# Down's weight sums formed block by block during gate and up, kept in DRAM, and loaded ready-made

## The chip, the cores and the metric

One Trainium2 chip, one core of it. The metric is the device time of one execution in microseconds (us); several executions are timed and their median is given. The kernel's engines are TensorE (PE, with its weight loads shown apart as PEld), VectorE (DVE), ScalarE (ACT), GpSimd (POOL) and SyncE (SP), whose queue issues nearly all DMAs.

## The reference

x is 2048 x 576, in float32. `a` is a linear attention of 32 heads of 18, `b` a gated MLP with 4608 inner columns, and the output mixes them row by row:

```python
g = sigmoid((x * gate_w).sum(-1, keepdims=True))
q, k, v = heads(x @ wqkv); pq, pk = phi(q), phi(k)      # phi(t) = (t + 1 if t > 0 else exp(t)) + 1e-6
kv = einsum("bhsd,bhse->bhde", pk, v); z = pk.sum(s)
a = merge((pq @ kv) / (pq . z + 1e-6)) @ wo
h = gelu(x @ w_gate) * (x @ w_up)                       # 2048 x 4608
b = h @ w_down                                          # 2048 x 576
out = g * a + (1 - g) * b
```

## The kernel before

Attention comes first, up to about 285 us of the profiled execution. Then follow two long stages with which the change deals.

**Gate and up** (to 1067.6 us). x and both weight matrices are cut in two halves along each side, and each product of 2 x 2 blocks is made with seven block products in place of eight. The work is 72 *chains*: for one pair of column blocks (n, 0 to 17), gate or up, and one half of the rows (p), the seven products. A product is one *step* of seven matmuls of 512 columns. Two neighbouring chains are interleaved: a *frame* is seven steps, `FRAME = 1, 7, 5, 3, 6, 2, 4`, of which steps 0, 4 and 5 belong to the chain that starts and steps 1, 2, 3 and 6 to the one before. The code of a step is issued in program order to all engines, and behind it whatever the dictionary `plan` holds for (frame, step); `put(frame, i, ...)` fills it. So `plan` sets the order on every queue. In it stand, among others:
- `fetch_at`: the load of the next raw weight blocks (768 KB into `wraw`, the front of the tile `stage`) and, behind it in the program, `weight_sums`: four subtractions on POOL (L373) that wait for this load.
- `split_at`: each block is split into a high part on ACT (L868) and a low part on POOL (L869, L870) for the float32r matmuls.
- `extras`: sums of finished h blocks (DVE, L996 and L999), stored to `h_d` in DRAM; `a`-side pieces go to `ha_d` and come back later.

Product 5 (`s5`, step 2 of a frame) ends with an ACT copy (L971) and a DVE addition that reads the bank `c` (L973 or L976); product 4 (`s4`, step 6) goes on accumulating in `c`.

**Down** (1067.6 us to the end). The table `DOWN` has 26 products; each has an h operand (`h_d`, a sum of h blocks) and a weight operand `v`, which is a block of w_down (a name of two digits) or a sum of blocks (a letter). Each product is done in three chunks, which makes 78 *units* of 36 matmuls of 288 columns, 18 in each half of a unit. A product marked `c` goes on in the PSUM banks of the one before. Behind a product's third chunk its banks are read into `acc` by DVE (L1403). Around each unit u the program issues, in this order: the first half's matmuls (and reads); `h_make(u + 3)`, which splits the raw h block (ACT L1240 or L1237, then DVE L1241 or L1238) and then loads another raw block into the buffer that this frees; `w_make(u + 3)`, which splits the weight operand (ACT L1203, POOL L1204); `w_sums`; the second half. At some u, `later()` does one more piece of the last chain's h sums (DVE L996, L999), with its stores and loads.

The class `Weights` keeps w_down blocks of 128 x 864 in up to 18 buffers `vt`. `fetch` loads blocks some units ahead (L1187), `sums(j)` forms the sums for unit j from them on DVE or POOL (L1198), and some sums stay in a buffer for later sums:

```python
        for name, x, op, y in DOWN[m].made:
            ...
            eng = nc.gpsimd if j > 4 and (c == 1 or c == 2 and m % 2) else nc.vector
            eng.tensor_tensor(self.tile(name, c), a, b, OP.add if op == "+" else OP.subtract)
```

Raw h blocks of 768 KB have three buffers (`raw_at`), and from a point in `later()` a fourth, `e123`, which until then serves the last chain's sums.

Of the kernel before, what the change touches and what calls it, by code (L numbers as in the profile page):

```python
# [8 lines left out]
F32 = mybir.dt.float32  # L9
# [76 lines left out]


class Product:

# [25 lines left out]
def tile_gated_mix(ctx, tc, xt, xs, xn, wk, wv, wq, wo, wgu, wdn, cst, out):  # L115
# [33 lines left out]
    class Scope:  # L149
        def __init__(self):  # L150
            self.stack = ExitStack()
# [994 lines left out]
    def raw_view(v):  # L1146
        return f32(v).rearrange("p (g c) -> p g c", g=3)

    wd = [wd_view(v) for v in (xf[:, 6144:7872], xf[:, 7872:9600], xf[:, 9600:11328], xf[:, 15936:17664])]
    hb = [h_view(v) for v in (xf[:, :3072], xf[:, 3072:6144], wf[1][:, :3072], xf[:, 12864:15936])]  # L1150
    raw_at = [raw_view(v) for v in (xf[:, 11328:12864], wf[0][:, :1536], wf[0][:, 1536:3072])] + [e123]
    raw_free = deque([0])
    vt = [stage[:, i * 864:(i + 1) * 864] for i in range(5)]

    class Weights:


        def __init__(self):
            self.tasks, self.last, self.at, self.free = [], {}, {}, list(range(15))
            used = {}  # L1160
            for j, (m, c) in enumerate(UNITS):
                d = DOWN[m]
                for name in [x for made in d.made for x in (made[1], made[3], made[0])] + [d.v]:
                    used.setdefault((name, c), []).append(j)
            self.spans = {}
            for (name, c), js in used.items():
                first = prev = js[0]
                for j in js[1:] + [10 ** 6]:
                    if j - prev > 9 and name.isdigit() or j == 10 ** 6:
                        self.spans.setdefault((name, c), []).append((first, prev))  # L1170
                        first = j
                    prev = j
            self.fetches = sorted((a, name, c) for (name, c), v in self.spans.items() for a, _ in v if name.isdigit())

        def tile(self, name, c):
            return vt[self.at[name, c]]

        def drop(self, j):
            for (name, c), v in self.spans.items():
                if (name, c) in self.at and any(b == j for _, b in v):  # L1180
                    self.free.append(self.at.pop((name, c)))

        def fetch(self, upto):
            while self.fetches and self.fetches[0][0] <= upto:
                _, name, c = self.fetches.pop(0)
                self.at[name, c] = self.free.pop(0)
                nc.sync.dma_start(self.tile(name, c).rearrange("p (g c) -> p g c", g=3),  # L1187
                                  wdn[2 * int(name[0]) + int(name[1])][:, 3 * c:3 * c + 3])

        def sums(self, j):  # L1190
            m, c = UNITS[j]
            for name, x, op, y in DOWN[m].made:
                dead = [k for k in (x, y) if any(b == j for _, b in self.spans[k, c]) and k != DOWN[m].v
                        and not any(k in (q[1], q[3]) for q in DOWN[m].made[DOWN[m].made.index((name, x, op, y)) + 1:])]
                a, b = self.tile(x, c), self.tile(y, c)
                self.at[name, c] = self.at.pop((dead[0], c)) if dead else self.free.pop(0)
                eng = nc.gpsimd if j > 4 and (c == 1 or c == 2 and m % 2) else nc.vector
                eng.tensor_tensor(self.tile(name, c), a, b, OP.add if op == "+" else OP.subtract)  # L1198

        def make(self, j):  # L1200
            m, c = UNITS[j]
            w, src = wd[j % 4], self.tile(DOWN[m].v, c)
# [4 lines left out]
    weight = Weights()  # L1207
    AHEAD = 3

    def w_sums(j, ahead=AHEAD):  # L1210
        if j < len(UNITS):
            weight.fetch(j + ahead)
            weight.sums(j)

    def w_make(j):
        if j < len(UNITS):
            weight.make(j)

# [89 lines left out]
    for n in range(3, NF2):  # L1308
        split_at(4 * n - 3, 0, GATE, *ALL)
        fetch_at(4 * n - 3, 5, n, UP)  # L1310
        split_at(4 * n - 1, 0, UP, *ALL)
        if n < NF2 - 1:
            fetch_at(4 * n - 1, 5, n + 1, GATE)
    for n, k in enumerate((1, 6, 2, 7, 5, 3, 4)):
# [15 lines left out]
    for do in late.pop(0):  # L1330
        put(LAST, 4, do)
    E_FREE = late.index([])
    late.pop(E_FREE)
# [33 lines left out]
    acc = dp.tile([128, 4, 2, 4, 288], F32, name="acc")  # L1367
    vt += [dp.tile([128, 864], F32, name=f"vt{i}") for i in range(10)]
    for v, k in ((f, 2), (sx, 1)):
        v = v.rearrange("p a b -> p (a b)")  # L1370
        vt += [v[:, i * 864:(i + 1) * 864] for i in range(k)]
    sets, set_of = [], {}
# [36 lines left out]
    def later():  # L1409
        if late:  # L1410
            for do in late.pop(0):
                do()
            if len(late) == 18 - E_FREE:
                raw_free.append(3)
            if not late:
                weight.free.extend((15, 16, 17))

    weight.fetch(7)
    acc_load(1)
    for u in range(len(UNITS)):  # L1420
        unit(u, 0)
        h_make(u + 3)
        w_make(u + 3)
        if not u:
            w_sums(4)
        w_sums(u + 5)
        unit(u, 1)
        if u in LATER:
            later()
        if u in (5, 12, 20):  # L1430
            acc_load((0, 2, 3)[(5, 12, 20).index(u)])
# [74 lines left out]
```

## Time and profile before

| | us |
|---|---|
| median of 3 runs (1453.39 to 1453.88) | 1453.6 |
| the profiled execution | 1452.77 |
| its span, first to last instruction | 1451.0 |
| DVE busy in the span | 989.0 |
| ACT busy | 640.8 |
| POOL busy | 823.6 |

The times of the prediction's rows are microseconds from the start of the span; the execution's own time is 1.77 us longer than its span, and the median of the runs is 0.83 us above the profiled execution. PE is busy for 1437.3 us of the span. A busy PE is not always PE at its pace, since a matmul's end is modelled; so the gaps are also read from the starts of the matmuls.

### The profile page before, as it was taken

Reading aid. Unit: us, or ns where it says so; the run is one execution under the profiler, and the core shown is the slowest. Engines: PE = TensorE matmul, PEld = TensorE weight load, DVE = VectorE, ACT = ScalarE, POOL = GpSimd, SP = SyncE. Lnnn points to the kernel's source line nnn. Section 1 sums busy time; section 2 is a strip of 40 time slices with the busy share of each in tenths; the row PEclk is TensorE's granted clock in tenths of the full one; section 3 lists DMA queues with packets and bytes.
Section 4 is the critical chain, followed back from the end, with each engine's and each line's share of the span. In section 5 each row is a group of like instructions: output and inputs, shape, how many; then the busy total and the mean of one; then the engine's idle time right before and its main releaser. Section 6 shows DMA issues by size and latency. Waiting matters only on the chain. (4 is left out here: it accounts for less than half of the span.)

```text
span 1451.0 us, 21113 instructions
## 1 busy us (share of the span) xinstructions
PE 1437.3 (99%) x8096; PEld 1281.7 (88%) x8096; DVE 989.0 (68%) x1115; ACT 640.8 (44%) x863; POOL 823.6 (57%) x511
## 2 busy tenths in 40 slices
PE   9999999999999999999999999999999999999999
PEld 9999899988888888888888888888889999999999
DVE  7887898343745538465374753647478989999794
ACT  7554656443333443333433334433345445444542
POOL 1674543365554545535445454455147968799895
PEclk9999999999999999999999999999999999999999
DMA  7574486663634436344263533535888787767771
GB/s 259 158 210 132 155 266 199 236 234 118 224 119 141 156 127 218 131 160 151 103 210 131 192 134 104 194 131 205 304 286 318 249 318 253 235 229 249 246 240 52
DMA packets 123925, 282.13 MB, mean 194 GB/s; under 512 B 12008, under 2 KB 39208, under 8 KB 122672
## 3 DMA queue, kind: packets, MB, share of 16 engines
q1 hardware_dynamic: 121232, 275.80, 55.7%
q10 hardware_dynamic: 2592, 4.98, 0.9%
q8 instruction: 63, 1.03, 0.3%
q14 instruction: 38, 0.31, 0.1%
HBM read 182.20 MB, written 98.50 MB: 193 GB/s over the span
## 5 line engine op out<-in xcount | busy, mean ns | idle before, releaser
L854 PE MATMUL bank<-xo,wg 128*128 128x512 f32 x1764 | 415.4, 389 | 0.5 <-ACT bank L943 0.5
L854 PE MATMUL bank<-xo,wu 128*128 128x512 f32 x1715 | 403.4, 389 | 0.0
L854 PEld LDWEIGHTS bank<-xo,wg 128*128 128x128 f32 x1764 | 330.8, 188 | 69.6 <-ACT bank L943 0.9
L854 PEld LDWEIGHTS bank<-xo,wu 128*128 128x128 f32 x1715 | 321.8, 188 | 67.0 <-DVE bank L976 0.2
L1393 PE MATMUL bank<-xo 128*128 128x288 f32 x2124 | 285.5, 295 | 5.4 <-DVE acc L1403 5.4
L1393 PEld LDWEIGHTS bank<-xo 128*128 128x128 f32 x2124 | 282.0, 188 | 6.9 <-DVE acc L1403 4.1
L373 POOL TENSOR_TENSOR stage<-stage 128x384 f32<-128x384 f32 x132 | 134.7, 1041 | 164.7 <-DMA stage<-wgu 162.0
L943 ACT ACTIVATE bank<-bank 128x512 f32<-128x512 f32 x139 | 80.9, 582 | 242.4 <-PE bank L854 237.2
L869 POOL TENSOR_TENSOR wg<-stage,wg 128x768 fp32r<-128x768 f32 (+3 forms) x41 | 73.9, 1802 | 126.9 <-ACT wg L868 122.3
L1204 POOL TENSOR_TENSOR xo<-vt,xo 128x864 fp32r<-128x864 f32 x42 | 124.2, 2965 | 27.9 <-ACT xo L1203 26.5
L1204 POOL TENSOR_TENSOR xo<-stage,xo 128x864 fp32r<-128x864 f32 x32 | 96.0, 3005 | 66.2 <-ACT xo L1203 66.2
L869 POOL TENSOR_TENSOR wu<-stage,wu 128x768 fp32r<-128x768 f32 (+2 forms) x36 | 74.0, 2056 | 86.2 <-ACT wu L868 81.9
L976 DVE TENSOR_TENSOR bank<-bank,mid 128x512 f32<-128x512 f32 x36 | 25.1, 697 | 143.2 <-ACT mid L971 143.1
L1393 PE MATMUL bank<-xo,wu 128*128 128x288 f32 x684 | 93.8, 295 | 1.4 <-DVE acc L1403 1.4
L1393 PEld LDWEIGHTS bank<-xo,wu 128*128 128x128 f32 x684 | 91.4, 188 | 1.9 <-DVE acc L1403 1.1
L973 DVE TENSOR_TENSOR f<-bank,mid 128x512 f32<-128x512 f32 x18 | 12.5, 692 | 115.0 <-ACT mid L971 110.8
L971 ACT ACTIVATE mid<-bank 128x512 f32<-128x512 f32 x71 | 42.4, 597 | 101.7 <-PE bank L854 90.3
L781 PEld LDWEIGHTS pair<-kw,p 128*128 128x128 f32 x448 | 60.8, 189 | 1.0
L781 PE MATMUL pair<-kw,p 128*128 128x288 f32 x448 | 61.4, 295 | 0.0
L531 PE MATMUL bank<-xo,qw 128*128 128x512 f32 (+1 forms) x231 | 55.7, 392 | 0.0
L1241 DVE TENSOR_TENSOR xo<-wg,xo 128x1536 fp32r<-128x1536 f32 x18 | 48.9, 2718 | 5.2 <-ACT xo L1240 5.2
L531 PEld LDWEIGHTS bank<-xo,qw 128*128 128x128 f32 (+1 forms) x231 | 41.9, 183 | 10.0
(257 smaller groups left out, 2190.6 us busy)
## 6 DMA issues: line engine op xcount, KB each, us to landing
wg<-h_d SPq DMA_DIRECT2D x41, 768.0 KB, 4.2
stage<-wgu SPq DMA_DIRECT2D x33, 768.0 KB, 5.0
h_d<-sx SPq DMA_DIRECT2D x72, 256.0 KB, 2.7
xo<-h_d SPq DMA_DIRECT2D x23, 768.0 KB, 4.2
h_d<-mid SPq DMA_DIRECT2D x64, 256.0 KB, 3.4
h_d<-e SPq DMA_DIRECT2D x63, 256.0 KB, 4.7
vt<-wdn SPq DMA_DIRECT2D x29, 432.0 KB, 5.2
e<-h_d SPq DMA_DIRECT2D x13, 768.0 KB
```

The lines of the kernel that those rows point to most:

```text
L373: nc.gpsimd.tensor_tensor(o, a, b, OP.subtract)
L531: nc.tensor.matmul(ps[:wa.shape[1]], wa, xa, start=(k == 0), stop=(k == len(ops) - 1), skip_group_check=g == 4)
L781: nc.tensor.matmul(y[:, i, :288], p[:, 5 * a + g], KW[g][:, wl, i * 288:(i + 1) * 288], start=(n == 0), stop=(n == 13))
L854: nc.tensor.matmul(ps, w_, x_, start=start and i == 0, stop=i == 6, skip_group_check=not start)
L869: nc.gpsimd.tensor_tensor(w[:, i, 3:5], src[:, :, 0:2], f32(w[:, i, 0:2]), OP.subtract)
L943: nc.scalar.activation(o, src, AF.Copy)
L971: nc.scalar.activation(d_sum, d, AF.Copy)
L973: nc.vector.tensor_tensor(es[3], ps["c"], d_sum, OP.add)
L976: nc.vector.tensor_tensor(d, ps["c"], d_sum, OP.add)
L1204: nc.gpsimd.tensor_tensor(w[:, 1], src, f32(w[:, 0]), OP.subtract)
L1241: nc.vector.tensor_tensor(h[:, 1], raw, f32(h[:, 0]), OP.subtract)
L1393: nc.tensor.matmul(y, h[:, hl, g, t * 128:(t + 1) * 128], w[:, wl, g * 288:(g + 1) * 288], start=first and c == 0 and n == 0, stop=c == NK ...
```

## The change

Each sum of w_down blocks is made during gate and up, for all products at once, in pieces. w_down's rows are in nine groups (`g`) of which a unit's weight operand uses three. For each g, a table `SUMS` of 48 steps makes 13 loads of 128 x 288 (144 KB; ten are pieces of blocks, three are sums that come back), forms 18 sums in five small buffers, and stores each to a DRAM tile `v_d` of its name. A word `4:2=0+1` means: at step 4, buffer 2 becomes buffer 0 plus buffer 1; `5:2>s` stores buffer 2 as `s`; `5:0<30` loads. The nine groups follow one another from frame 4 to frame 65. That adds 117 loads, 162 stores and 162 sums there, 79 of the sums on DVE and 83 on POOL. The buffers are the rear of `stage` and a new tile `fifth`.

In down, `Weights` is gone. Each unit's operand is loaded from `wdn` or `v_d` into one of five buffers (`v_fetch`), five units ahead, issued behind `w_make` of the unit that had the buffer. The room of the other `vt` buffers goes to raw h blocks: `e123` is no longer one of them, and five buffers `hr` come in one by one behind units 5, 6, 8, 10 and 11.

Two smaller edits: from n = 3 on, `weight_sums` is issued three steps behind its load and no longer right behind it; the first down loads of the old kernel (blocks for units up to 3 at frame LAST - 4, step 6) become the operands of units 0 to 4 at the same place.

```diff
+SUMS = """
+0:0<11 0:1<31 0:3<21 4:2=0+1 5:2>s 5:0<30 6:4=3-1 7:4>y 7:3<10 9:2=0+2 10:2>t 11:4=4-0 12:4>r 13:2=3+2
...
+"""
...
+    v_d = {name: dram.tile([128, NF2 // 2, 288], F32, name=f"v_d{name}") for name in "yrvwzoxkmqpnsjutAl"}
...
+    fifth = stages.tile([128, 320], F32, name="fifth")
...
-    raw_at = [raw_view(v) for v in (xf[:, 11328:12864], wf[0][:, :1536], wf[0][:, 1536:3072])] + [e123]
+    raw_at = [raw_view(v) for v in (xf[:, 11328:12864], wf[0][:, :1536], wf[0][:, 1536:3072])]
...
-    class Weights:
...
+    class Sums:
+        def __init__(self, g):
+            self.g, self.slots = g, [stage[:, c:c + 288] for c in range(3072, 4224, 288)] + [fifth[:, :288]]
...
+        def do(self, what, eng):
+            o, s, g = self.slots[int(what[0])], self.slots, self.g
+            if what[1] == "<":
+                nc.sync.dma_start(o, v_at(what[2:])[:, g])
+            elif what[1] == ">":
+                nc.sync.dma_start(v_at(what[2:])[:, g], o)
+            else:
+                eng.tensor_tensor(o, s[int(what[2])], s[int(what[4])], OP.add if what[3] == "+" else OP.subtract)
+
+    def v_fetch(j):
+        if j < len(UNITS):
             m, c = UNITS[j]
...
+            nc.sync.dma_start(vt[j % 5].rearrange("p (g c) -> p g c", g=3), v_at(DOWN[m].v)[:, 3 * c:3 * c + 3])
+
+    def w_make(j):
+        if j < len(UNITS):
+            w, src = wd[j % 4], vt[j % 5]
             nc.scalar.activation(w[:, 0], src, AF.Copy)
             nc.gpsimd.tensor_tensor(w[:, 1], src, f32(w[:, 0]), OP.subtract)
-            self.drop(j)
...
+            v_fetch(j + 5)
...
+        for m, frame, blocks in ((GATE, 4 * n - 3, (n, UP)), (UP, 4 * n - 1, (n + 1, GATE))):
+            split_at(frame, 0, m, *ALL)
+            if blocks[0] < NF2:
+                put(frame, 5, lambda at=blocks: nc.sync.dma_start(wraw, wgu[at]))
+                put(frame + 1, 1, lambda: weight_sums(wraw, tsum))
+    for g in range(NF2 // 2):
+        one = Sums(g)
+        for at, what in one.tasks():
+            frame, i = divmod(28 + 48 * g + at, 7)
+            eng = nc.gpsimd if i > 3 or frame % 2 == 0 == i else nc.vector
+            put(frame, i, lambda one=one, what=what, eng=eng: one.do(what, eng))
...
-    for frame, i, do in ((LAST - 4, 6, lambda: weight.fetch(3)), (LAST - 2, 1, lambda: h_direct(0)),
+    for frame, i, do in ((LAST - 4, 6, lambda: [v_fetch(j) for j in range(5)]), (LAST - 2, 1, lambda: h_direct(0)),
...
-                         (LAST + 1, 6, lambda: (h_make(2), weight.sums(3)))):
+                         (LAST + 1, 6, lambda: h_make(2))):
...
-    vt += [dp.tile([128, 864], F32, name=f"vt{i}") for i in range(10)]
...
+    raw_at += [raw_view(dp.tile([128, 1536], F32R, name=f"hr{i}")) for i in range(5)]
...
-    weight.fetch(7)
+    MORE = 5, 6, 8, 10, 11
     acc_load(1)
     for u in range(len(UNITS)):
         unit(u, 0)
         h_make(u + 3)
         w_make(u + 3)
-        if not u:
-            w_sums(4)
-        w_sums(u + 5)
         unit(u, 1)
+        if u in MORE:
+            raw_free.append(3 + MORE.index(u))
+            h_load()
```

How the order moves, at three places. On DVE in down around unit 18, before: the split of an h block (L1241), a weight sum (L1198), one of the last chain's sums (L996), the next split, the reads of a product (L1403).

```order
L1403 SCALAR_TENSOR_TENSOR acc<-bank,gate,acc 128x288 x2
L1241 TENSOR_TENSOR wu<-xo,wu 128x1536
L1198 TENSOR_TENSOR vt_8788<-stage,vt_8788 128x864
L996 TENSOR_TENSOR e_3256<-e_3256,r 128x512
L1241 TENSOR_TENSOR xo<-wg,xo 128x1536
L1403 SCALAR_TENSOR_TENSOR acc<-bank,gate,acc 128x288 x2
L1241 TENSOR_TENSOR xo<-wg,xo 128x1536
```

And now, where L1222 is the split, L1005 the sum of h blocks and L1386 the read:

```order
L1386 SCALAR_TENSOR_TENSOR acc<-bank,gate,acc 128x288 x2
L1222 TENSOR_TENSOR wu<-hr_9246,wu 128x1536
L1005 TENSOR_TENSOR e_3274<-e_3274,r 128x512
L1222 TENSOR_TENSOR xo<-xo 128x1536
L1386 SCALAR_TENSOR_TENSOR acc<-bank,gate,acc 128x288 x2
L1222 TENSOR_TENSOR xo<-hr_9249,xo 128x1536
```

The weight sum is gone from between them; nothing else has changed its place there.

On SP's queue in the last two frames of gate and up, before: weights of the last chain (`xo<-wp_d`), pieces of the `a` side to be kept (`ha_d`), and the raw h block of unit 2 (`wu<-h_d`).

```order
L1318 DMA xo<-wp_d_97 128x640
L1011 DMA ha_d8x<-sx 128x512
L1011 DMA ha_d8y<-f 128x512
L1318 DMA xo<-wp_d_97 128x640
L1011 DMA ha_d_151<-sx 128x512
L1223 DMA wu<-h_d_100 128x1536
L1318 DMA xo<-wp_d_97 128x640
L1011 DMA ha_d_152<-f 128x512
```

And now, with L1305 for the weights, L1020 for the pieces, L1204 for the raw h block:

```order
L1305 DMA xo<-wp_d_97 128x640
L1020 DMA ha_d8x<-sx 128x512
L1020 DMA ha_d8y<-f 128x512
L1191 DMA stage<-wdn 128x864
L1305 DMA xo<-wp_d_97 128x640
L1020 DMA ha_d_151<-sx 128x512
L1204 DMA wu<-h_d_100 128x1536
L1305 DMA xo<-wp_d_97 128x640
L1020 DMA ha_d_152<-f 128x512
```

A load of 432 KB (L1191, the operand of unit 6) has come in; that of unit 5 stands a few rows ahead of these, that of unit 7 a few rows behind.

On DVE in a frame of gate and up (frame 35), before: the last chain's sums, then the addition that reads bank `c` (L973).

```order
L996 TENSOR_TENSOR sx<-bank,sx 128x512
L999 TENSOR_TENSOR e_3256<-f,e_3256 128x512
L996 TENSOR_TENSOR e_3256<-e_3256,r 128x512
L973 TENSOR_TENSOR e_3256<-bank,mid 128x512
L983 TENSOR_TENSOR e_3256<-bank,mid 128x512
L996 TENSOR_TENSOR sx<-r,f 128x512
```

And now, L982 being that addition and L1186 a sum of the new table:

```order
L1005 TENSOR_TENSOR sx<-bank,sx 128x512
L1008 TENSOR_TENSOR e_3274<-f,e_3274 128x512
L1186 TENSOR_TENSOR stage<-stage 128x288
L1005 TENSOR_TENSOR e_3274<-e_3274,r 128x512
L982 TENSOR_TENSOR e_3274<-bank,mid 128x512
L992 TENSOR_TENSOR e_3274<-bank,mid 128x512
L1186 TENSOR_TENSOR fifth<-fifth,stage 128x288
L1005 TENSOR_TENSOR sx<-r,f 128x512
```

Two sums of 128 x 288 have come in, one of them two rows ahead of the addition.

More of the change, by code (lines that the diff above doesn't have):

```diff
@@ L1150, in tile_gated_mix @@
     hb = [h_view(v) for v in (xf[:, :3072], xf[:, 3072:6144], wf[1][:, :3072], xf[:, 12864:15936])]
-    raw_at = [raw_view(v) for v in (xf[:, 11328:12864], wf[0][:, :1536], wf[0][:, 1536:3072])] + [e123]
+    raw_at = [raw_view(v) for v in (xf[:, 11328:12864], wf[0][:, :1536], wf[0][:, 1536:3072])]
     raw_free = deque([0])
     vt = [stage[:, i * 864:(i + 1) * 864] for i in range(5)]
-    class Weights:
[L1158 to L1190, printed above, removed]
-            m, c = UNITS[j]
[L1192 to L1202, printed above, removed]
@@ new lines, in v_at, with tasks @@
+    def v_at(name):
+        return wdn[2 * int(name[0]) + int(name[1])] if name.isdigit() else v_d[name]
+    class Sums:
+        def __init__(self, g):
+            self.g, self.slots = g, [stage[:, c:c + 288] for c in range(3072, 4224, 288)] + [fifth[:, :288]]
+        def tasks(self):
+            for word in SUMS.split():
+                at, what = word.split(":")
+                yield int(at), what
+        def do(self, what, eng):
[6 more added lines that the diff above has]
+                eng.tensor_tensor(o, s[int(what[2])], s[int(what[4])], OP.add if what[3] == "+" else OP.subtract)
@@ L1215, in w_make @@
-    def w_make(j):
-        if j < len(UNITS):
-            weight.make(j)
+            v_fetch(j + 5)
     DIRECT = 3
@@ L1331, in tile_gated_mix @@
         put(LAST, 4, do)
-    E_FREE = late.index([])
-    late.pop(E_FREE)
+    late.remove([])
     for k, src, (frame, i), (back, j) in kept:
@@ L1412, in later @@
                 do()
[L1413 to L1416, printed above, removed]
-    weight.fetch(7)
+    MORE = 5, 6, 8, 10, 11
     acc_load(1)
```

17 lines of the change are left out of this document (3 added, 14 removed).

## The prediction

> **What bounds the kernel now.** I read the page's head first, then each stage's busy times, then who waits for PE's banks, then PE's timeline.
>
> ```profile
> span 1451.0 us, 21113 instructions
> PE 1437.3 (99%) x8096; PEld 1281.7 (88%) x8096; DVE 989.0 (68%) x1115; ACT 640.8 (44%) x863; POOL 823.6 (57%) x511
> ...
> 600.00:690.00 90.00, 90.00 (x399) 74.53 (x398) 49.71 (x66) 33.72 (x48) 45.67 (x35) 1.00 0.46 152
> ...
> 1150.00:1200.00 50.00, 47.76 (x357) 47.01 (x356) 44.85 (x28) 24.47 (x24) 33.49 (x12) 1.00 0.87 311
> ...
> PE bank L1393 <- DVE acc L1403: 6.8, 8, 1.8
> ...
> PE bank L854 <- DVE bank L976: 0.9, 1, 0.9
> ```
>
> The columns of a stage row are length, then busy PE, PEld, DVE, ACT, POOL, the granted clock, the DMA share and GB/s. Only PE bounds: in gate and up it is busy 90.00 of 90.00 us with DVE and POOL half idle, so nothing there can be gained. In down DVE is busy 44.85 of 50 us and PE loses 2.24. The rows of the waits name the cause: eight times PE waits for DVE's read of a product (L1403). PE's timeline gives the price:
>
> ```profile
> 1067.60 9.65 PE L1393 MATMUL bank<-xo 128*128 128x288 f32 x72
> ...
> 1157.35 2.61 PE L1393 MATMUL bank<-xo,wu 128*128 128x288 f32 x18 [0.58 <-DVE acc L1403]
> 1160.78 2.65 PE L1393 MATMUL bank<-xo,wu 128*128 128x288 f32 x18 [0.83 <-DVE acc L1403]
> ...
> 1414.40 14.40 PE L1393 MATMUL bank<-xo 128*128 128x288 f32 x108
> 1428.64 4.91 PE L1393 MATMUL bank<-xo,wu 128*128 128x288 f32 x36
> 1433.39 14.40 PE L1393 MATMUL bank<-xo 128*128 128x288 f32 x108
> ```
>
> Undisturbed, 108 matmuls take 1428.64 - 1414.40 = 14.24 us, so a unit of 36 takes 4.75 and half a unit 2.37. From 1157.35 to 1160.78 half a unit took 3.43: the stall cost 1.06, 0.23 more than its idle 0.83. Eight stalls make 6.8 + 8 x 0.23 = 8.6 us. The whole checks it: from the first unit (1067.60) to the 76th (1433.39) there are 2700 matmuls, at 14.24 per 108 they take 356.0, and they took 365.8: 9.8 us lost. The 1.2 between I cannot place and do not count.
>
> **What the change takes away in down.** Is a weight sum the reason that DVE reads late?
>
> ```profile
> 1148.90 2.77 DVE L1241 TENSOR_TENSOR wu<-xo,wu 128x1536 fp32r<-128x1536 f32 x1
> 1151.59 2.91 DVE L1198 TENSOR_TENSOR vt<-stage,vt 128x864 f32<-128x864 f32 x1
> 1154.42 0.68 DVE L996 TENSOR_TENSOR e<-e,r 128x512 f32<-128x512 f32 x1
> 1155.02 1.75 DVE L1241 TENSOR_TENSOR xo<-wg,xo 128x1536 fp32r<-128x1536 f32 x1
> 1156.69 0.93 DVE L1403 SCALAR_TENSOR_TENSOR acc<-bank,gate,acc 128x288 f32<-128x288 f32 x2
> ...
> 1067.00:1451.00 384.00, 68.64 (x27) 89.47 (x27) 1.00 0.69 240
> ...
> 1059.27 1.47 ACT L1237 ACTIVATE xo<-xo 128x1536 fp32r<-128x1536 f32 x1
> ...
> 1224.68 3.61 DVE L1238 SCALAR_TENSOR_TENSOR wu<-wg,wu 128x1536 fp32r<-128x1536 f32 x1
> 1228.22 2.55 DVE L999 TENSOR_TENSOR r<-sx,r 128x512 f32<-128x512 f32 x1
> 1230.68 1.78 DVE L1403 SCALAR_TENSOR_TENSOR acc<-bank,gate,acc 128x288 f32<-128x288 f32 x4
> ```
>
> At the stall of 1157.35 DVE had no gap from 1148.90 on. Without the 2.91 us sum the first reads would have begun 2.9 us sooner, where 0.82 was missing. The stage row (length, DVE, POOL) is of L1198 alone: 27 sums with 68.6 us on DVE and 27 with 89.5 on POOL, all of which leave. Over the 26 products that is 2.6 us of DVE for each product of 14.24; the longest stall is 1.8. So I take the 8.6 back, less what other late work leaves. The worst place is the product with two destinations for each bank (1230.68, four reads in 1.78 us), with no sum right ahead of it but a piece of the last chain's sums (2.55). There, at worst and without the sums, ACT's copy (1.47), the split beside POOL (3.61), the piece beside POOL (2.55), the reads of two banks (1.78), the next split bare (1.75, as at 1155.02) and the third bank's two reads (0.9) end 12.1 us after the unit began in which the copy stands; PE wants that bank after 2.5 units, 11.9. I leave 0.2 there and 0.4 for the rest: 0.6 in all. The bounds are 0 and 4.3 (half the stalls stay). Down: +8.0.
>
> **What it adds in down.** 78 operand loads of 432 KB in place of 48 block loads; with a raw h block (768 KB) each 4.75 us, 1.229 MB or 259 GB/s. Units 5 to 11 (33 us) also bring five extra h blocks and one `acc_load` (1.18 MB): 5.1 MB, 154 GB/s more, 413 in all.
>
> ```profile
> 1110.00:1120.00 10.00, 10.00 (x78) 10.00 (x77) 9.36 (x9) 5.01 (x6) 8.54 (x3) 1.00 1.04 403
> ```
>
> 403 GB/s is the fullest that this trace shows for so long; 413 leaves a backlog of 0.3 MB, under 1 us, and the last chain's pieces perhaps 2 us more. An operand is loaded five units (23.7 us) ahead, an h block three units (14.2) less about 5 for DVE's split and SP's turn. Hidden; without cover the cost is the backlog itself. A page speaks against this: the Trainium skill, "DMA: Bandwidth & Descriptors", section Specifications, gives a core about 358 GB/s of HBM. By it the backlog would be 55 GB/s x 33 us = 1.8 MB or 5 us (an estimate), still inside 9 us of lead, and 403 in the row above says the limit does not hold here.
>
> `v_fetch` puts a wait for POOL's low part (L1204) on SP. Behind it stand the h loads and the stores of the last chain's pieces; all have a lead of units, so it costs nothing unless POOL falls behind by two units, and POOL loses 89 us of work here.
>
> **What it adds at the junction.** Operands 5, 6 and 7 are now loaded in the last two frames of gate and up; the old kernel loaded four blocks only after them. The queue is full there (a stage row with its DMA share of 1.02, then rows of the SP, DVE, ACT and PE timelines):
>
> ```profile
> 1045.00:1050.00 5.00, 5.00 (x24) 4.14 (x23) 4.93 (x7) 3.37 (x4) 0.57 (x1) 1.00 1.02 372
> ...
> 1055.35 0.38 SPq L1011 DMA_DIRECT2D ha_d<-f  x1
> ...
> 1056.67 0.69 DVE L983 TENSOR_TENSOR f<-bank,mid 128x512 f32<-128x512 f32 x1 [1.37 <-DMA ha_d8y<-f]
> ...
> 1058.75 0.57 ACT L943 ACTIVATE bank<-bank 128x512 f32<-128x512 f32 x1
> ...
> 1064.01 0.60 ACT L932 ACTIVATE f<-bank 128x512 f32<-128x512 f32 x1 [3.27 <-DMA ha_d<-f]
> 1064.51 0.59 ACT L971 ACTIVATE mid<-bank 128x512 f32<-128x512 f32 x1
> ...
> 1065.13 0.70 DVE L976 TENSOR_TENSOR bank<-bank,mid 128x512 f32<-128x512 f32 x1 [1.92 <-ACT mid L971]
> ...
> 1065.88 1.88 PE L854 MATMUL bank<-xo,xo 128*128 128x512 f32 x7 [0.90 <-DVE bank L976]
> ```
>
> ACT's gelu at 1064.01 overwrites `f[2]` and waits for its store, issued at 1055.35 and done 8.6 us later; behind it on ACT stands the copy that DVE needs, and behind that PE, 0.90 us late already. Operands 5 and 6 (0.885 MB) go ahead of this store. At 372 GB/s that is 2.4 us; part falls into the short dip at 1053 when SP waits for DVE, and I take 1.9. Each us that the store is later goes straight to PE. Bounds: 0 (were the queue not FIFO) and 3.0 (also operand 5 delaying `ha_d8y`, so L983 and the seed L943 that PE needs at 1060.1). By the 358 GB/s of that page the two loads would take 2.5 us (an estimate), the sum hardly differs. Junction: -1.9.
>
> **What it adds in gate and up.** 79 sums on DVE, 83 on POOL, 279 DMAs of 144 KB (41 MB over 680 us, 60 GB/s beside the 152). The slack is read from the frame that stands third in the order (rows of the timelines, a group, a DMA issue with its KB and us to landing):
>
> ```profile
> 654.14 0.60 ACT L971 ACTIVATE mid<-bank 128x512 f32<-128x512 f32 x1 [0.20 <-PE bank L854]
> ...
> 652.89 2.23 DVE L996 TENSOR_TENSOR e<-e,r 128x512 f32<-128x512 f32 x1
> 655.04 0.68 DVE L973 TENSOR_TENSOR e<-bank,mid 128x512 f32<-128x512 f32 x1
> ...
> 649.12 11.27 PE L854 MATMUL bank<-xo,wg 128*128 128x512 f32 x49
> 660.22 1.75 PE L854 MATMUL bank<-xo,wu 128*128 128x512 f32 x7
> ...
> 661.17 0.37 SPq L858 DMA_DIRECT2D stage<-wgu  x1
> ...
> L373 POOL TENSOR_TENSOR stage<-stage 128x384 f32<-128x384 f32 x132 | 134.7, 1041 | 164.7 <-DMA stage<-wgu 162.0
> ...
> out<-acc SPq DMA_DIRECT2D x32, 144.0 KB, 5.0
> ```
>
> Seven steps take 660.22 - 649.12 = 11.10, a step 1.59. L973 ends at 655.72; product 4 starts one step ahead of 660.22, at 658.63: 2.9 us of slack in a DVE-heavy frame. No row shows a 128 x 288 sum on two SBUF operands; by elements, L996 bare (0.68 for 512) gives 0.4, and one that meets POOL (2.23) up to 2. On POOL, L373 gives 0.8. A load stands four steps (6.3 us) or more ahead of its sum; 144 KB land in about 5, and SP runs late by up to 661.17 - 658.63 = 2.5. So a sum may wait 1.2 and take 0.4 to 2: 1.6 to 3.2 against 2.9. SP's added waits for sums hold up the weight load behind them; POOL's subtractions now follow their load by three steps, and POOL idled 162 us for it. So nothing reaches PE in most frames: 0, bounds 0 and -9 (rival C). A lock rule agrees with the price: "SBUF — State Buffer", section "SBUF: two separate sides", in the Trainium skill, says that one of DVE and GpSimd holds the shared port for its whole instruction; the sum by it is the upper end, 2.
>
> **Sum.** 8.0 - 1.9 + 0 = 6.1 us from the profiled 1452.77: 1446.7. The median stands 0.83 above that execution: 1453.6 - 6.1 = 1447.5.
>
> **Rivals.**
> A, the loads at the junction are hidden: with 5 and 6 behind the store in effect, or the store already landed with its bytes read, only the 8.0 counts: 1445.6. The 8.6 us that the store took speaks against.
> B, down's stalls stay in part: the backlog or late pieces of the last chain keep half of the 8.6, and the junction costs 1.9: 1453.6 - 4.3 + 1.9 = 1451.2. For it: DVE is still busy with 2.7 us splits beside POOL; against: no stall in the last 150 us, where sums were made too but no such pieces.
> C, gate and up begins to stall, the slower side: DVE, in order, waits at a sum for its late load ahead of L973 or L976, and product 4 waits for that. At worst load lag 2.5 + 5 - 6.3 = 1.2, sum 2, the order's next L996 again 1.5 later than now: 4.7 against 2.9, 1.8 a time; once in each of nine groups costs 16, half of that 8: 1447.5 + 8 = 1455.5 and more. It decides when lag passes 2.9 in over six frames. For it: SP's queue is filled with waits for sums. Against: 5 us to landing is the row at the busy end, and most sums meet idle DVE.
> D, the sums do not leave the path: they do leave DVE's queue, by the order; no chance of its own.
>
> **Numbers.** Forecast 0.52 (1446.0 to 1449.5), A 0.16, B 0.16, C 0.16. A measurement tells 0.2%, 2.9 us. Faster: forecast, A, and a little of B, 0.70. Same: most of B and a mild C, 0.16; slower: 0.14. The range runs from 1444.0 (nothing lost, the 0.9 at the junction gone) to 1454.5 (into C, the rest of which is left out).
>
> **What would show it.** Right: no row of PE waiting for the reads in down, 4.75 us units from 1067 on; the gelu at the junction waiting 5 us, not 3.3, and PE about 2.8, not 0.9; PE 90.00 of 90.00 in gate and up. Wrong: PE rows with gaps from L973's or L976's successor before 1000 us, POOL or DVE waiting there for `stage<-wdn`; or ACT's copy of an h block waiting for its DMA in units 5 to 15.

## The result, and the profile after

| | before | after |
|---|---|---|
| median of 6 runs, us | 1453.4 (1452.6 to 1453.9) | 1466.1 (1460.5 to 1468.8) |
| ratio | | 1.0084, 95% from 1.0066 to 1.0101 |
| profiled execution, us; span; granted clock | 1452.8; 1451.0; 1.000 | 1465.0; 1463.1; 0.997 |
| first unit of down starts, us | 1067.60 | 1089.46 |
| first to 76th unit (2700 matmuls), us | 365.8 | 356.0 |

The kernel is 0.84% slower, and the forecast was 1447.5. Down gave back all that it could; what comes before it lost 21.9 us. The page's head, and the one row of its waits that is new, show it (engine, line, what was waited for: us in total, times, longest):

```profile
span 1463.1 us, 21813 instructions
PE 1441.9 (99%) x8096; PEld 1284.4 (88%) x8096; DVE 960.3 (66%) x1166; ACT 638.1 (44%) x863; POOL 794.7 (54%) x568
...
PE bank L863 <- DVE e L982: 14.7, 7, 3.6
```

DVE is less busy than before (66% of the span, not 68%) and yet PE now waits for it. PE's timeline has the seven waits about 90 us apart, one in each eight frames; here are the first, the second with what follows it, and the last:

```profile
395.11 3.36 PE L863 MATMUL bank<-xo,wg 128*128 128x512 f32 x7 [2.46 <-DVE e L982]
...
489.18 2.22 PE L863 MATMUL bank<-xo,wg 128*128 128x512 f32 x7 [3.38 <-DVE e L982]
491.19 3.06 PE L863 MATMUL bank<-xo,wu 128*128 128x512 f32 x7
494.09 4.98 PE L863 MATMUL bank<-xo,wg 128*128 128x512 f32 x21
...
947.08 1.88 PE L863 MATMUL bank<-xo,wg 128*128 128x512 f32 x7 [1.31 <-DVE e L982]
```

A step of seven matmuls takes 1.59 us. Behind the pause of 3.38 us the two steps took 491.19 - 489.18 = 2.01 and 494.09 - 491.19 = 2.90, so the pause cost 1.73 us more than itself. The stage rows of the same kernel (length, then busy PE, PEld, DVE, ACT, POOL, the granted clock, DMA share, GB/s) name the reason, the granted clock:

```profile
420.00:510.00 90.00, 86.62 (x375) 71.24 (x374) 50.74 (x68) 32.76 (x47) 50.38 (x43) 0.98 0.64 209
...
490.00:495.00 5.00, 5.00 (x16) 3.97 (x15) 1.99 (x4) 2.81 (x5) 1.99 (x2) 0.66 0.94 289
```

After the stalls of 2.46, 3.38 and 3.58 us the next two steps took 1.66, 1.73 and 1.73 us too long, 5.1 together; after the four stalls of 0.80 to 1.66 us they did not. So of the 21.9 us 14.7 are waiting and 5.1 a slower clock. The rest, about 2, is mostly the restart behind each stall (some 0.3 us behind each of the four small ones), and small differences elsewhere.

Why is DVE late just there? The profile of the kernel before had the answer, in two stage rows that the prediction does not use:

```profile
545.00:570.00 25.00, 25.00 (x112) 20.69 (x111) 24.52 (x32) 8.40 (x13) 14.14 (x10) 1.00 0.74 253
570.00:600.00 30.00, 30.00 (x134) 24.84 (x133) 12.77 (x18) 10.19 (x15) 14.29 (x11) 1.00 0.40 131
```

For 25 us of each 89 (eight frames) DVE had next to no idle time: 24.52 of 25.00 here, and 24.3 to 24.7 in each of the seven such stretches from 366 to 927 us. The L973 (now L982) for which PE waits stands at the end of that stretch. In the 30 us behind it DVE was busy for 12.77. The 90 us row quoted in the prediction averages the two. In the changed kernel four to eight sums stand in each of seven such stretches, and one in an eighth: 41 in all, 25 of them on DVE. (Of all 162 sums DVE does 78 and POOL 84, not 79 and 83.) DVE's timeline ahead of the second stall, and then POOL's at the first of these sums:

```profile
460.90 2.33 DVE L1186 TENSOR_TENSOR stage<-stage 128x288 f32<-128x288 f32 x1
...
475.48 0.49 DVE L1186 TENSOR_TENSOR stage<-stage 128x288 f32<-128x288 f32 x1 [2.46 <-DMA stage<-wdn]
...
484.77 1.36 DVE L1186 TENSOR_TENSOR stage<-stage 128x288 f32<-128x288 f32 x1
486.06 1.74 DVE L1008 TENSOR_TENSOR e<-f,e 128x512 f32<-128x512 f32 x1
...
488.45 0.68 DVE L982 TENSOR_TENSOR e<-bank,mid 128x512 f32<-128x512 f32 x1
```

```profile
460.51 2.41 POOL L878 TENSOR_TENSOR wg<-stage,wg 128x1024 fp32r<-128x1024 f32 x1
```

Three sums (2.33, 0.49, 1.36) and one wait for a load (2.46) make 6.6 us, 3.7 more than the slack of 2.9; the stall is 3.38. A sum by itself takes 0.45 us. The one at 460.90 took 2.33: POOL was splitting weights (L878) from 460.51 to 462.92, and the sum ended right behind that, at 463.23.

At the junction, ACT's gelu and PE (two timelines), and then PE's first and last units in down:

```profile
1085.87 0.60 ACT L941 ACTIVATE f<-bank 128x512 f32<-128x512 f32 x1 [2.26 <-DMA ha_d<-f]
```

```profile
1087.74 1.88 PE L863 MATMUL bank<-xo,xo 128*128 128x512 f32 x7 [0.43 <-DVE bank L985]
1089.46 9.65 PE L1376 MATMUL bank<-xo 128*128 128x288 f32 x72
...
1445.46 14.40 PE L1376 MATMUL bank<-xo 128*128 128x288 f32 x108
```

The gelu waits 2.26 us for its store, not 3.27, and PE 0.43, not 0.90. In down, PE runs 2700 matmuls in 1445.46 - 1089.46 = 356.0 us without a wait.

### The profile page after: what moved, and what is told of

Same layout as the page of the kernel before. It is cut to its first block, busy times and chain, and to the rows that moved or that the text cites. A ratio compares the mean times of both kernels' runs of the same rounds, so it can differ in the third digit from the quotient of the medians.

```text
span 1463.1 us, 21813 instructions
## 1 busy us (share of the span) xinstructions
PE 1441.9 (99%) x8096; PEld 1284.4 (88%) x8096; DVE 960.3 (66%) x1166; ACT 638.1 (44%) x863; POOL 794.7 (54%) x568
## 4 chain that ended last, share of the span: by engine, by line
PE 80%; DVE 10%; DMA 6%; issue 2%; SPq 1%; ACT 1%; POOL 1%; DVEq 0%; ACTq 0%; POOLq 0%
PE bank L863 39%; PE bank L1376 25%; PE bank L540 4%; PE pair L790 3%; DVE sx L1005 2%; PE pair L343 2%; DMA stage<-wdn 2%; PE pair L298 2%; PE kpair L343 2%; PE kpair L298 2%; DVE e L1005 1%; DMA stage<-wgu 1%; DVE e L945 1%; DMA fifth<-wdn 1%; DVE stage L1186 1%
## 5 line engine op out<-in xcount | busy, mean ns | idle before, releaser
L863 PE MATMUL bank<-xo,wg 128*128 128x512 f32 x1764 | 419.8, 391 | 15.2 <-DVE e L982 14.7
L1197 POOL TENSOR_TENSOR xo<-stage,xo 128x864 fp32r<-128x864 f32 x78 | 210.6, 2700 | 197.2 <-ACT xo L1196 190.1
L382 POOL TENSOR_TENSOR stage<-stage 128x384 f32<-128x384 f32 x132 | 139.1, 1075 | 187.5 <-DMA stage<-wgu 184.8
L878 POOL TENSOR_TENSOR wg<-stage,wg 128x768 fp32r<-128x768 f32 (+3 forms) x41 | 73.9, 1802 | 76.1 <-ACT wg L877 72.3
L878 POOL TENSOR_TENSOR wu<-stage,wu 128x768 fp32r<-128x768 f32 (+2 forms) x36 | 75.8, 2106 | 38.5 <-ACT wu L877 35.9
L1196 ACT ACTIVATE xo<-stage 128x864 fp32r<-128x864 f32 x78 | 71.1, 911 | 0.0
L982 DVE TENSOR_TENSOR f<-bank,mid 128x512 f32<-128x512 f32 x18 | 12.4, 692 | 87.1 <-ACT mid L980 82.4
L1186 DVE TENSOR_TENSOR stage<-stage 128x288 f32<-128x288 f32 x58 | 54.5, 940 | 22.9 <-DMA stage<-wdn 9.9
L1186 POOL TENSOR_TENSOR stage<-stage 128x288 f32<-128x288 f32 x59 | 55.3, 938 | 14.4 <-DVE r L1008 4.2
```

The source lines that it names most:

```text
L382: nc.gpsimd.tensor_tensor(o, a, b, OP.subtract)
L863: nc.tensor.matmul(ps, w_, x_, start=start and i == 0, stop=i == 6, skip_group_check=not start)
L878: nc.gpsimd.tensor_tensor(w[:, i, 3:5], src[:, :, 0:2], f32(w[:, i, 0:2]), OP.subtract)
L1186: eng.tensor_tensor(o, s[int(what[2])], s[int(what[4])], OP.add if what[3] == "+" else OP.subtract)
```

## The experiments

Theory 1: sums that stand in the full stretch make L982 late by the time they take on DVE. Theory 2: DVE stands at sums for late loads. Rival 3: POOL's operations hold DVE up, so a sum costs DVE as much from POOL. Rival 4: the added transfers and the clock are the loss. The last column, of the profiled execution alone, tells where the loss arose: down took 356.0 us from its first to its 76th unit in all of these profiles but two (358.0 in the runs "all on DVE" and "one sum", in which 108 undisturbed matmuls of down take 14.32 us and not 14.24; why stays open).

| run | median, us | ratio to before, 95% | first unit of down, us |
|---|---|---|---|
| all sums on POOL | 1491.9 | 1.0264 (1.0248 to 1.0279) | 1117.84 |
| full frames' sums on POOL | 1458.6 | 1.0036 (1.0023 to 1.0049) | 1083.92 |
| no sums | 1445.5 | 0.9944 (0.9928 to 0.9961) | 1069.23 |
| sums without loads | 1459.7 | 1.0041 (1.0026 to 1.0055) | 1083.87 |
| sums placed anew, first | 1455.9 | 1.0018 (1.0006 to 1.0030) | 1080.68 |
| POOL's queue | 1506.6 | 1.0354 (1.0334 to 1.0374) | 1125.47 |
| all sums on DVE | 1470.4 | 1.0102 (1.0081 to 1.0122) | 1095.20 |
| longer leads | 1466.2 | 1.0090 (1.0074 to 1.0107) | 1090.72 |
| narrower stretch | 1471.0 | 1.0128 (1.0111 to 1.0145) | 1094.32 |
| no sums in the full stretch | 1444.4 | 0.9944 (0.9930 to 0.9958) | 1067.04 |
| two places kept free | 1445.2 | 0.9946 (0.9934 to 0.9959) | 1069.19 |
| one sum in each stretch | 1448.9 | 0.9961 (0.9948 to 0.9974) | 1074.45 |

### No sums

```
-            else:
+            elif g == 0:
                 eng.tensor_tensor(o, s[int(what[2])], s[int(what[4])], ...)
```

> The sums of the groups 1 to 8 are left out (144 of 162), so most of down's operands are not the right sums; their loads and stores stay where they are and move what they moved. Theories 1 and 2 and rival 3 (the sums themselves): no stall behind L982, 1443 to 1446. Rival 4 (the transfers, SP's longer queue or the moved sums of gate's and up's own blocks): the stalls stay, 1458 or more.

Measured: 1445.5 us. With every load and store in its place the loss is gone, so the transfers, SP's longer queue and the moved sums of gate's and up's own blocks cost no more than about 1 us. (The sums of group 0 are still there, and with them one stall of 1.07 us.) Rival 4 falls.

### Sums without loads

```
             if what[1] == "<":
-                nc.sync.dma_start(o, v_at(what[2:])[:, g])
+                if g == 0:
+                    nc.sync.dma_start(o, v_at(what[2:])[:, g])
```

> The loads of the groups 1 to 8 are left out (104 of 117), so their sums run over what stands in the buffers: as many sums in the same places, with no load to wait for; the stores stay. Theory 1 (occupied time: a DVE sum takes 0.63 us and more beside POOL): most of the loss stays, 1455 to 1464. Theory 2 (waiting for late loads): the stalls go, 1443 to 1448. Rival 3 (POOL's port): as theory 1. Rival 4 (transfers): between, as two thirds of the added traffic are gone here, 1445 to 1455.

Measured: 1459.7 us. Of the 1466.1 - 1445.5 = 20.6 us that the sums cost, 14.2, some 70%, stay when no sum has a load to wait for. PE's waits alone go from 14.7 to 11.0 us, and the clock falls twice and not three times. So the time that the sums take is the larger part, as theory 1 says; rival 3 gave the same range, and this run does not tell them apart.

### All sums on POOL

```
-            eng = nc.gpsimd if i > 3 or frame % 2 == 0 == i else nc.vector
+            eng = nc.gpsimd
```

> All sums of weight blocks go to POOL; loads, stores and their places stay. Without the seven PE stalls behind L982 (21.5 us with what follows them) the changed kernel's 1466.1 would be about 1444.6; the 9.8 us that down gave back stay. Theory 1 (DVE's queue of the fullest two frames in eight has no idle time, so each sum that stands there makes L982 later): no stall, 1443 to 1447. Theory 2 (DVE stands at a sum for its late load, 9.9 us in all): the same here. Rival 3 (POOL's operations hold DVE up on their common port, so a sum costs DVE as much from POOL): half of the stalls or more stay, 1453 to 1460. Rival 4 (the added transfers and the lower clock are the loss): nothing changes, 1462 or more.

Measured: 1491.9 us, 26 us above the change, which none of the theories had said. Waits of DVE and of SP's queue between 300 and 1070 us:

```profile
DVE mid L1008 <- DMA mid<-ha_d: 46.2, 22, 6.3
...
DVE e L982 <- DMA h_d<-e: 23.5, 5, 6.4
...
SPq L1184 <- POOL stage L1186: 258.5, 63, 11.1
SPq L1184 <- POOL fifth L1186: 85.4, 23, 8.5
```

SP issues in the order of the program. It stood 344 us at stores (L1184) of sums that POOL, busy or waiting for a block load, had not made. Behind them stood the `get` loads of `ha_d` pieces that DVE needs, and DVE stood 46.2 us for those, and 23.5 us more at L982 for stores (`h_d<-e`) of the same queue. Moving work off a full engine made that engine wait through a third one. Call this theory 5: SP's order.

### The full frames' sums on POOL

```
-            eng = nc.gpsimd if i > 3 or frame % 2 == 0 == i else nc.vector
+            eng = nc.gpsimd if i > 3 or frame % 2 == 0 == i or frame % 8 in (2, 3) else nc.vector
```

> Only the sums that stand in the frames numbered 2 and 3 modulo 8 (the two ahead of each stall; 18 of DVE's 79) go to POOL; the other 61 stay on DVE. Theory 1 (only what stands in the full frames counts): stalls nearly all gone, 1443 to 1448. Theory 2 (late loads anywhere in DVE's order, since the delay is handed on): most of the waits for loads stay in other frames, so half of the stalls stay, 1452 to 1458. Rival 3 (POOL holds DVE up): 1455 or more. Rival 4 (transfers): 1462 or more.

Measured: 1458.6 us, above the ranges of theories 1 and 2 and in that of rival 3; five stalls, 9.5 us. (The edit moves 18 of DVE's 78 sums, so 60 stay.) DVE's timeline ahead of the largest (3.92 us):

```profile
570.54 0.69 DVE L1008 TENSOR_TENSOR mid<-mid,bank 128x512 f32<-128x512 f32 x1 [3.99 <-DMA mid<-ha_d]
```

DVE had caught up and then waited 3.99 us for a `get` load; in the chain of waits that load was issued by SP right behind a store whose sum POOL made at 566.20, after its block sums (L382). So the run tells less than it was meant to: the sums' time left DVE, but ahead of this stall theory 5's wait came in its place. That the other four stalls have the same cause is not shown.

### Loads and stores from POOL's own queue

As "all sums on POOL", with both `nc.sync.dma_start` of `do` turned into `nc.gpsimd.dma_start`.

> As the run with all sums on POOL (1491.9), but the loads and stores of the sums are issued from POOL's own queue and no longer from SP's. Theory 5 (there SP stood 344 us at stores whose sums POOL hadn't made, and DVE waited 46 us for `get` loads behind them): the `get` loads are early again and most of the 47 us go, 1445 to 1460. Rival 3 (POOL itself is late with its splits, or holds DVE up on their port): nothing is gained, 1480 or more.

Measured: 1506.6 us, worse still. Waits of PE and DVE, a stage row, and a group of POOL's (busy us, mean ns):

```profile
PE bank L863 <- POOL wu L878: 18.4, 13, 3.1
...
DVE mid L1008 <- DMA mid<-ha_d: 3.9, 4, 1.7
...
510.00:600.00 90.00, 84.95 (x366) 67.76 (x366) 52.99 (x63) 30.84 (x45) 78.81 (x85) 1.00 0.62 208
...
L1182 POOL DMA_DIRECT2D stage<-wdn x66 | 35.8, 543 | 12.3 <-DMA v_du<-stage 4.3 <-DMA v_dm<-stage 3.6 <-issue 3.6
```

DVE's wait for `ha_d` did go, from 46.2 to 3.9 us, which is what theory 5 says of its mechanism. But to issue a transfer takes POOL 0.54 us, POOL is now busy for 78.81 of 90 us, and its splits (L878) reach PE late. So the first half of rival 3 (POOL itself is late) took the gain.

### All sums on DVE

```
-            eng = nc.gpsimd if i > 3 or frame % 2 == 0 == i else nc.vector
+            eng = nc.vector
```

> All 162 sums on DVE at the places they have in the change. Theory 1 (time taken on DVE in the full frames): six or seven sums in place of three or four stand in each full stretch, 2 us more of 0.63 each at all eight, and the stall is longer by that: 1470 to 1485. Theory 5 (the sums that wait behind POOL's other work are what holds SP and DVE): with DVE's sums made in time SP's queue is earlier, 1452 to 1464.

Measured: 1470.4 us, at the lower edge of theory 1's range, but not by what theory 1 gives. With 41 sums on DVE in the full stretches in place of 25, each stall was to be about 2 us longer; the same seven stalls have 17.8 us in place of 14.7, and 2.0 us of what the profiled execution lost lie in down, where no sums stand. More sums on DVE cost little more. That fits rival 3, by which a sum costs DVE time from POOL too, but DVE's waits for loads changed as well, and no run separates the two.

### No sums in the full stretch

```
-                put(frame, i, ...)
+            if what[1] in "<>" or not 8 <= frame % 8 * 7 + i < 24:
+                put(frame, i, ...)
```

> The change with the 41 sums (25 of them DVE's) left out that stand in the 16 steps of each eight frames in which DVE had no idle time (so many of down's operands are not the right sums); the other 121 sums, all loads and all stores stay in their places. Theory 1: no stall behind L982 in any full stretch, 1443 to 1447. Theory 2 (delays handed on from sums in other frames, and waits for loads): stalls of over 1 us stay at half the stretches, 1450 to 1460.

Measured: 1444.4 us. The sum over seven stages of 90 us, from 330 to 960, and waits of DVE from 300 to 1070 us:

```profile
sum 630.00, PE 630.00 PEld 521.85 DVE 390.71 ACT 236.41 POOL 378.87; mean PE 90.00 PEld 74.55 DVE 55.82 ACT 33.77 POOL 54.12
...
DVE stage L1186 <- DMA stage<-wdn: 9.0, 5, 2.8
DVE fifth L1186 <- DMA v_dy<-fifth: 7.6, 2, 4.3
DVE stage L1186 <- DMA v_dt<-stage: 6.1, 1, 6.1
```

PE is busy for 630.00 of 630.00 us, as before the change, while 121 sums run where they ran and DVE still stands at some of them for up to 6.1 us. Where these 121 stand, a sum and even its wait cost nothing; the 41 sums inside the full stretch are the whole loss. (Not every place outside it is free, as the runs with sums placed anew show.) So it is theory 1, with theory 2 only inside the stretch. How the loss divides between DVE's 25 sums there, with their waits, and POOL's 16 this run does not show.

### One sum in each stretch

As the run above, but the first of DVE's sums in each stretch stays.

> As the run without the 41 sums of the full stretches (1444.4), but with the first of DVE's sums in each of the eight stretches kept (8 of 162; the other 33 are left out, so many of down's operands are not the right sums). The prediction reckoned with one sum for each stretch against 2.9 us of slack: by it one sum of 0.63 to 2.33 us fits, no stall of over 0.5 us and 1443 to 1446. If the slack was less than that, a stall of 0.5 to 2 us comes at most of the eight, 1450 to 1456.

Measured: 1448.9 us, between the two ranges. PE's waits, and DVE's timeline ahead of one of them:

```profile
PE bank L863 <- DVE e L982: 3.6, 4, 1.2
```

```profile
459.52 2.33 DVE L1186 TENSOR_TENSOR stage<-stage 128x288 f32<-128x288 f32 x1
...
479.37 0.69 DVE L1008 TENSOR_TENSOR mid<-mid,bank 128x512 f32<-128x512 f32 x1 [1.48 <-DMA mid<-ha_d]
```

Four stalls of 0.8 to 1.2 us where the prediction's count allowed none. One sum nearly fits. At each of the four the sum met POOL and took 2.3 us of the 2.9, and DVE then waited 1.0 to 1.5 us for the `get` load into `mid`: what DVE finishes late also frees `mid` late. In three of the other stretches the sum took 0.45 to 0.51 us and nothing stalled; in the last it took 2.33 but the wait was only 0.30. So the slack is near the 2.9 that the prediction read, and several sums cannot fit.

### Sums placed anew

The loop over `one.tasks()` works out the places itself: the same sequence, all sums on DVE, none in steps 8 to 23 of 56, at most one a step.

```
+                at = max(s_ready[u], s_ready[v], s_prev + 1, 0 if o in (u, v) else s_free[o])
+                while 8 <= at % 56 < 24:
+                    at += 1
...
+            put(*divmod(at, 7), lambda one=one, what=what: one.do(what, nc.vector))
```

> The same 162 sums, loads and stores in the same sequence, all sums on DVE, with their places worked out anew: none in the 16 steps of each eight frames in which DVE had no idle time before the change (step 1 of frame 1 to step 2 of frame 3, modulo 8), at most one a step elsewhere, three steps or more after its load, the stores a step after. Theory 1 (only time taken in the full frames counts, since elsewhere DVE is idle for about half): no stall behind L982, 1443 to 1447, faster than both. Theory 2 (late loads hand a delay on): waits for loads stay in the light frames and are made up there, the same. Theory 5, new from the two runs with more sums on POOL (SP works in order, stands at the store of a sum that isn't made, and the `get` loads of later sums stand behind it): the stores still stand ahead of the `get` loads, so DVE's L1008 waits for its piece and half of the loss stays, 1450 to 1458.

Measured: 1455.9 us. No stall in the full stretch, but four elsewhere. The number lies in theory 5's range, but by luck: in this trace no L1008 waits for its `ha_d` piece. DVE ahead of the first, and PE:

```profile
403.29 0.87 DVE L1186 TENSOR_TENSOR fifth<-fifth,stage 128x288 f32<-128x288 f32 x1 [5.61 <-DMA v_dy<-fifth]
```

```profile
404.82 2.59 PE L863 MATMUL bank<-xo,wg 128*128 128x512 f32 x7 [1.85 <-DVE f L982]
```

The sum overwrites a buffer whose store stood behind a block load of 768 KB. I took such waits for the rest of the loss and gave these transfers more lead (`s_over` is the step from which a sum may overwrite a buffer; steps 12, 13 and 0 of 14 are those at and behind a block load):

```
-                s_ready[o] = at + (4 if any(s % 14 == 12 for s in (at - 2, at - 1, at)) else 3)
+                s_ready[o] = at + 2 + 3 * (at % 14 in (12, 13, 0))
...
+                s_free[o], s_over[o] = max(s_free[o], at + 2), max(s_over[o], at + 2 + 3 * (at % 14 in (12, 13, 0)))
...
-                while 8 <= at % 56 < 24:
+                while 9 <= at % 56 < 24:
```

> As the run with the sums placed outside the full frames (1455.9), with one thing more: a load or a store that is issued within three steps of a block load of gate and up (768 KB; in that run what stood behind it landed up to 7 us later) gets five steps and not two or three until a sum reads or overwrites its buffer. The remaining four stalls of that run each followed a DVE sum that stood 4.3 to 5.6 us for such a transfer. If that wait is the rest of the loss: no stall of over 1 us, 1444 to 1447, faster than both. If the rest is the time that the sums take on DVE or SP's order: about 1455 again.

Measured: 1466.2 us; that was wrong, or at least not all. The edit also does more than the expectation says: away from block loads the lead falls from three steps to two, and step 8 is no longer kept free. So it is no test of the leads alone. PE's waits and its first and last stall, and DVE's timeline ahead of the first:

```profile
PE bank L863 <- DVE e L982: 15.0, 7, 3.1
...
440.57 1.89 PE L863 MATMUL bank<-xo,wg 128*128 128x512 f32 x7 [2.88 <-DVE e L982]
...
990.86 2.25 PE L863 MATMUL bank<-xo,wg 128*128 128x512 f32 x7 [3.07 <-DVE e L982]
```

```profile
434.64 2.62 DVE L1186 TENSOR_TENSOR stage<-stage 128x288 f32<-128x288 f32 x1 [3.13 <-DMA stage<-v_ds]
```

Seven stalls again, 92 us apart, but half a period from the former ones: there is a second L982 in each eight frames at which DVE has little to spare, and the new places had put sums of 1.2 to 2.7 us, some with waits of up to 3.1, just ahead of it. The next run keeps only steps 10 to 22 free and gives a load three steps, and two more near a block load:

> As the run above, but only 13 steps of 56 are kept free of sums in place of 15 (step 1.2 ahead of the full stretch and 3.2 at its end may hold one), and the loads' lead is a step longer. Theory 1 (taken time in the full stretch): a sum at 1.2 costs 0.6 to 2.3 us there, so stalls of 1 to 2 us come back at several of the eight stretches: 1448 to 1456. Theory 2 (late loads and stores alone): the same as the run above or better, 1443 to 1447.

Measured: 1471.0 us, above both ranges, with stalls at both places, one of 6.1 us. A load's longer lead does not help as long as sums stand there. So the last version keeps both places free (leads of two steps, and two more near a block load):

```
-                while 9 <= at % 56 < 24:
+                while 9 <= at % 56 < 24 or 47 <= at % 56 < 52:
```

> The sums placed anew once more, all on DVE: none in 15 steps of the full stretch (1.2 to 3.2 modulo 8) and none in five steps (6.5 to 7.2) ahead of a second L982 of the same eight frames, where the two runs before had all or most of their stalls; a load or store near a block load has two steps more of lead. Theory 1 in its narrower form (what counts is a sum that stands on DVE, by its own time or by its wait, within a few us ahead of one of those two L982): no stall of over 1 us, 1444 to 1448, faster than both kernels. If instead it is the crowding of all 162 sums on DVE, wherever they stand, or SP's queue: stalls at other places, 1453 to 1466.

Measured: 1445.2 us, ratio 0.9946 (0.9934 to 0.9959) to the kernel before: it beats both. The sum over the same seven stages:

```profile
sum 630.00, PE 629.44 PEld 520.56 DVE 450.71 ACT 235.88 POOL 321.07; mean PE 89.92 PEld 74.37 DVE 64.39 ACT 33.70 POOL 45.87
```

DVE does all 162 sums and is busy for 451 us there, 60 more than in the run without the 41 sums, and PE loses 0.6. With all sums on DVE and at other places, 1466.1 has become 1445.2; with all on DVE at the change's own places it was 1470.4.

## Why the prediction was wrong, step by step

- **Down, +8.0: right, 9.8 came.** All eight stalls went, and with them the 1.2 us that I could not place and the 0.6 that I held back. The added loads were hidden; no row of PE's waits names down. Which part the added buffers for h blocks have in it, beside the sums that left, no run separates.
- **Junction, -1.9: wrong, about +0.5.** PE waits 0.43 there, not 2.8. I took the store's 8.6 us for a queue in front of it that two more loads would lengthen one for one. The queue was as full as said, but the store landed 7.7 us after its issue (1078.21), and the gelu waited less. Rival A, hidden, was the right reading; no run takes these loads away, so why the store was no later stays open.
- **Gate and up, 0: the step that failed; about -22.4 came** (the 21.9 lost ahead of down, and the junction's 0.5). It held one sum ("a sum may wait 1.2 and take 0.4 to 2") against the 2.9 us of slack at one L973. Both numbers stand: the slack is near that, as the run with one sum shows, and a sum takes 0.45 to 2.6. But the slack is shared by the whole stretch of 25 us in which DVE hardly idles, and the table puts four to eight sums there, two to five of them on DVE. "Most sums meet idle DVE" was true, 121 of 162 stand outside these stretches, and no help: those cost nothing, the other 41 cost everything. The prediction took the frame's end and left out how long DVE had been without a gap before it.
- **Rival C named the place and the mechanism at 0.16, and priced them too low**: 8 us, up to 16, where 21.9 came. It reckoned with one sum of 2 us, the wait of 1.2 for its load and 1.5 from the next L996, once in each group; two to five sums on DVE stand in seven stretches. In the run without loads 70% of the loss stays, and 5.1 us are the clock that falls behind the longer pauses, which had no term.
- What I named as signs were the right ones: the gaps of PE at L982 before 1000 us showed it at once.

Beside the row with the 2.33 us sum stands the rule that the prediction cited from the Trainium skill, "SBUF — State Buffer", section "SBUF: two separate sides": one of DVE and GpSimd holds the shared port for its whole instruction. The trace agrees, 0.45 us bare and 2.33 beside POOL's split.

## What to carry to other kernels

Before work is added to an engine that is half idle, fold its timeline by the period of the loop and look for stretches in which it has no gap at all: the slack at the end of such a stretch is one allowance for all that is put into it. Work outside it can be free even where it waits, as the 121 sums were, but not everywhere: here there was a second place with little to spare. An engine that issues transfers in order is such a queue too, and moving work from one engine to another can make it the one that waits. Then place by phase: here the same 162 sums, all on DVE, gave 1470.4, 1466.2 or 1445.2 us by where they and their transfers stand.

## What was not expected of the hardware

PE's granted clock falls after pauses shorter than I expected, and not after all of them. Two pairs of stage rows: around the pause of 1.85 us that ends at 404.82 in the first run with the sums placed anew, and around the pause of 2.88 us that ends at 440.57 in the run with longer leads:

```profile
402.33:405.74 3.41, 1.56 (x7) 0.98 (x6) 2.45 (x4) 0.63 (x1) 2.80 (x3) 1.00 0.32 112
405.74:409.15 3.41, 3.41 (x10) 2.66 (x9) 1.39 (x3) 1.72 (x3) 1.65 (x2) 0.50 0.45 135
```

```profile
435.82:439.23 3.41, 1.86 (x9) 1.21 (x7) 3.41 (x3) 0.00 (x0) 2.49 (x2) 1.00 0.00 0
439.23:442.65 3.42, 2.08 (x9) 1.74 (x10) 2.25 (x5) 2.10 (x4) 0.00 (x0) 1.00 0.78 259
```

The clock is 0.50 behind the shorter pause and 1.00 behind the longer. The difference is where the pause lies. Up to the last matmul, every fall of the clock in these traces lasts 3.41 us or twice that, and within one trace the falls lie whole multiples of 3.41 us apart (in the changed kernel they begin at 394.98, 490.56 and 674.88, 28 and 54 multiples apart). Cut into stretches of 3.41 us by that rhythm, the shorter pause lies whole in one of them and the longer is divided into 1.55 and 1.34. Over all traces the clock fell 27 times. By the matmuls' modelled ends, a stretch in which PE was idle for 2.0 us or more always had a fall behind it, one with less than 1.75 never, and between the two it went either way.

The Trainium skill, "TensorE: Matmul & The Clock Gate", Part 1, has the clock go to half after an idle window of about 3.4 us, in windows that run freely, whatever the kernel does. That the windows run freely, and their length, agree with these rows; that a pause of 1.85 us, little more than half a window, can be enough does not. A price for a stall of about 1.8 us or more should hold some 1.7 us (3.41 us at half the clock) for it, as a part that may or may not come.

To issue a transfer cost POOL 0.54 us of its own time, as the group in the run with POOL's queue shows.
